# A fused linear-attention and feed-forward kernel: the first two chunks of a batch as one unit with two neighbouring tokens per partition

## The chip, the cores and the metric

The kernel runs on one core of one Trainium2 chip. The metric is the device time in microseconds of one execution. The core has TensorE (matmuls; in the profile PE, and PEld for its weight loads), VectorE (DVE), ScalarE (ACT), GpSimd (POOL) and SyncE (SP), which work side by side and wait for each other by semaphores, and 16 DMA engines that move data between device memory and the on-chip memory. Matmuls write to eight accumulator banks, from which VectorE or ScalarE copy.

## The reference

Two stages follow each other. The first is a recurrence over 768 tokens for 4 batches and 8 heads of 48 channels, all inputs fp32:

```
state = zeros((B, H, D, D))
for t in range(S):                       # S = 768, B = 4, H = 8, D = 48
    cur   = einsum('bhd,bhe->bhde', u * k[t], v[t])
    y[t]  = einsum('bhd,bhde->bhe', r[t], state + cur)
    state = w[t][:, :, :, None] * state + einsum('bhd,bhe->bhde', k[t], v[t])
```

The second takes y as 3072 tokens of 384 features and multiplies: `a = x @ w1`, `b = x @ w2`, `h = (a * b) @ w3`, `out = h @ w_out`, with a hidden width of 1024. The decay w lies between 0.8 and 0.95.

## The kernel before

The tokens of a batch are cut into six chunks of 128. Inside a chunk the recurrence is done as matmuls: with the running sum of log w over the chunk (`cs`, a matmul with a triangular matrix LT), k is scaled by exp(-sum) and r by exp(+sum), both are transposed so that channels lie on partitions, their product (`m`) is masked to earlier tokens (`msk`, or a copy and a select, `mcp` and `maff`), and multiplied with v (`yi`). The state that came into the chunk adds its part (`ys`), the token's own term is a row sum (`rk`, `ruk`, `dg`) times v (`dv`), added by VectorE (`yb`) or by a matmul with the identity (`yd`, for units in Y_PE). At the end of a chunk the state becomes (old state + k^T v) times the chunk's decay (`kv`, `T`, `S`, and a bf16 copy `Sb`).

A unit is one chunk of one or two batches, as listed in `UNITS` by chunk, first batch and number of batches; before there are thirteen, the first two of one batch. The tokens of the chunk lie on the 128 partitions, batches and heads side by side. `loads` (L337 to L354) brings r, k, v and w of a unit with four transfers; a row of one head and token is 48 fp32 values, 192 bytes. GpSimd's queue converts r, k and v to bf16 on the way; unit 0 comes unconverted over the queues of SP and ScalarE and is cast (`rc`, `kc`, `vc`, L349). In the units of the set RAW the sums are formed in transposed order by matmuls too (`csT`, L493) and r is transposed as it was loaded (`trw`, L505, then `KRw`, L510); in the others r is scaled first (`iw`, `rw`, `KRr`). Transposes are matmuls with the identity, or transfers on SP's queue where the unit stands in DMA_R, DMA_K or DMA_Y.

The feed-forward stage needs `w34 = w3 @ w_out`, built in eight pieces during the start (`wt`, `w3Te`, `wm`, `w34e`). Each unit's y, transposed as `xT`, is a block: `a` and `b` (L729) in four groups, ScalarE copies a (L734), VectorE multiplies (L739), and `o` (L745) gives 128 output rows, copied (L750) and stored by SP (L755).

The order of all work is written out by hand in `ORDER`, as names with an engine; each engine takes its own in that order and waits inside it. `BANKS` gives each product its accumulator bank. GpSimd's queue carries the loads after unit 0, the weights (w3 in quarters, w1 and w2 in halves, wo whole) and some computing, in the order of the list; a transfer of this queue waits for the landing of the one eight before it. `warmN@n` puts n/4 matmuls with zeros into TensorE's queue. Up to the first FFN product the order of transfers on GpSimd's queue is:

```
win_2 rin_1 kin_1 vin_1 win_3 kin_3 kin_2 rin_2 rin_3 w3_0 w3_1 wo win_4 vin_3 vin_2 w3_2 win_5 rin_4 w1_1
kin_4 rin_5 w2_1 kin_5 w1_0 win_6 w2_0 ...
```

Of the kernel before, what the change touches and what calls it, by code (L numbers as in the profile page):

```python
# [13 lines left out]
UNITS = [(0, 0, 1), (0, 1, 1), (0, 2, 2), (1, 0, 2), (1, 2, 2), (2, 0, 2), (2, 2, 2), (3, 0, 2), (3, 2, 2), (4, 0, 2),  # L14
    (4, 2, 2), (5, 0, 2), (5, 2, 2)]
# [13 lines left out]
RAW = {0, 1, 2, 3, 6}  # L29
N_PSUM = set()  # L30
DEPTH = {}
BLOCKS = [(0,), (1,), (2,), (3,), (4,), (5,), (6,), (7,), (8,), (9,), (10,), (11,), (12,)]
ROW_PC = {10}
DMA_R = {7, 8, 9, 10, 11, 12}
DMA_K = {8, 9, 10, 11, 12}
DMA_Y = {8, 9, 10, 11, 12}
PE_DIAG = set()
F32_IN = {0}
POOL_MASK = {(2, 0), (4, 1), (7, 1), (9, 1)}
Y_PE = {0, 1}  # L40
# [23 lines left out]
ORDER = """
zeros@DVE kin_0@ACT win_0@SP padlw@DVE ones@DVE win_1@ACT u@SP padpx@DVE I128@POOL padkr@DVE table@ACT rin_0@SP
padr@POOL vin_0@ACT win_2@POOL kc_0@DVE LT@POOL ln_0@ACT rin_1@POOL warm0@34 csT_0@PE cs_0@PE kin_1@POOL rc_0@DVE
ne_0@ACT vin_1@POOL ln_1@ACT KRk_0@DVE uc@DVE et_0@ACT warm2@13 trk_0@PE mask@DVE win_3@POOL cs_1@PE vc_0@ACT warm4@3
cc_1@PE csT_1@PE trw_0@PE cc_0@PE kin_3@POOL ln_2@ACT ne_1@ACT warm6@20 cs_2@PE kin_2@POOL et_1@ACT rk_1@DVE warm0@3
cc_2@PE pc_1@ACT ub@PE KRk_1@DVE trw_1@PE rk_0@DVE ue@ACT trk_1@PE rin_2@POOL pc_0@ACT ne_2@ACT ruk_0@DVE trke_0@DVE
padet@DVE KRw_1@DVE rin_3@POOL KRw_0@DVE ln_3@ACT warm0@29 m_0_0@PE w3_0@POOL kv_0@PE kv_1@PE msk_0_0@DVE trke_1@ACT  # L70
w3_1@POOL warm2@6 csT_2@PE S_0@DVE m_1_0@PE et_2@ACT dg_0@DVE wo@POOL dv_0@DVE pc_2@ACT win_4@POOL ruk_1@DVE warm0@12
csT_3@PE dg_1@DVE cs_3@PE KRk_2@DVE cc_3@PE vin_3@POOL msk_1_0@DVE pc_3@ACT trk_2@PE ne_3@ACT et_3@ACT vin_2@POOL
rk_2@DVE trw_3@PE dv_1@DVE yi_1_0@PE trw_2@PE trke_2@DVE w3_2@POOL yi_0_0@PE yd_1@PE KRk_3@DVE yd_0@PE ybc_1@ACT
win_5@POOL KRw_3@DVE ybc_0@ACT warm0@7 yt_1@PE trk_3@PE Sb_0@ACT KRw_2@DVE xT_1@ACT wt_1_0@PE rin_4@POOL trke_3@ACT
S_1@DVE wt_1_1@PE ruk_2@DVE m_2_0@PE m_2_1@PE Sb_1@ACT mcp_2_0@ACT wt_0_0@PE msk_2_1@DVE wt_0_1@PE w1_1@POOL m_3_1@PE
w3Te_0@ACT wt_2_0@PE msk_3_1@DVE yt_0@PE wt_2_1@PE xT_0@ACT m_3_0@PE w3Te_1@ACT maff_2_0@DVE warm2@1 ys_3@PE wt_3_0@PE
dg_2@DVE wt_3_1@PE rk_3@DVE ruk_3@DVE kin_4@POOL warm7@16 wm_1@PE msk_3_0@DVE wm_0@PE w3Te_3@DVE ln_4@ACT rin_5@POOL
dg_3@DVE w34e_1@ACT wm_3@PE iw_4@ACT w3Te_2@DVE w2_1@POOL w34e_0@DVE yi_3_0@PE dv_3@POOL w34e_3@ACT cs_4@PE yi_3_1@PE
e_4@ACT yi_2_0@PE wm_2@PE ne_4@ACT dv_2@POOL yb_3@DVE yi_2_1@PE w34e_2@DVE kv_3@PE kv_2@PE kin_5@POOL yb_2@DVE
wt_4_0@PE cc_4@PE wt_4_1@PE pc_4@ACT wt_5_0@PE w3Te_4@DVE yt_3@PE w1_0@POOL yt_2@PE xT_3@ACT S_2@DVE wt_5_1@PE wm_4@PE  # L80
win_6@POOL w3Te_5@DVE ln_5@ACT Sb_2@ACT cs_5@PE rw_4@DVE w2_0@POOL wm_5@PE e_5@ACT T_3@DVE KRr_4@DVE xT_2@ACT S_3@DVE
trr_4@PE iw_5@ACT w34e_4@DVE win_7@POOL cc_5@PE a_2_3@PE pc_5@ACT trre_4@ACT a_1_1@PE KRk_4@DVE vin_4@POOL a_2_2@PE
w34e_5@ACT a_3_3@PE asb_2_2@ACT rw_5@DVE kin_6@POOL trk_4@PE ne_5@ACT KRr_5@DVE a_0_1@PE trke_4@ACT rk_4@DVE a_3_2@PE
ruk_4@DVE asb_1_1@ACT w3_3@POOL trr_5@PE asb_0_1@ACT b_1_1@PE asb_2_3@ACT b_2_2@PE KRk_5@DVE win_8@POOL b_2_3@PE
rk_5@DVE abT_2_2@DVE b_0_1@PE abT_2_3@DVE asb_3_2@ACT trk_5@PE vin_5@POOL abT_0_1@DVE a_2_1@PE abT_1_1@DVE b_3_2@PE
asb_2_1@ACT trke_5@DVE m_4_0@PE ln_6@ACT win_9@POOL m_4_1@PE trre_5@DVE a_0_0@PE mcp_4_1@ACT msk_4_0@DVE a_1_0@PE
cs_6@PE rin_6@POOL abT_3_2@DVE asb_1_0@ACT b_0_0@PE asb_0_0@ACT ruk_5@DVE cc_6@PE ne_6@ACT a_3_1@PE dg_4@DVE b_1_0@PE
pc_6@ACT kin_7@POOL ln_7@ACT abT_0_0@DVE a_3_0@PE asb_3_1@ACT abT_1_0@DVE asb_3_3@ACT b_2_1@PE dv_4@POOL asb_3_0@ACT
cs_7@PE abT_2_1@DVE Sb_3@ACT m_5_0@PE ys_4@PE e_7@ACT maff_4_1@POOL msk_5_0@DVE kv_4@PE yi_4_0@PE a_2_0@PE rin_8@POOL
T_4@DVE cc_7@PE asb_2_0@ACT yi_4_1@PE csT_6@PE yb_4@DVE ne_7@ACT b_2_0@PE rin_7@POOL iw_7@ACT KRk_6@DVE wt_6_0@PE  # L90
yt_4@PE abT_2_0@DVE b_3_3@PE S_4@POOL pc_7@ACT xT_4@ACT dg_5@DVE wt_6_1@PE wt_7_0@PE win_11@POOL w3Te_6@ACT b_3_0@PE
abT_3_3@DVE a_4_1@PE abT_3_0@DVE ln_8@ACT kin_10@POOL wt_7_1@PE wm_6@PE et_6@ACT w3Te_7@DVE vin_7@POOL dv_5@DVE
asb_4_1@ACT cs_8@PE w34e_6@ACT vin_6@POOL ys_5@PE ln_9@ACT m_5_1@PE kv_5@PE msk_5_1@DVE yi_5_0@PE ne_8@ACT a_4_3@PE
win_10@POOL iw_8@ACT cc_8@PE rk_6@DVE yi_5_1@PE trw_6@PE asb_4_3@ACT KRk_7@DVE kin_8@POOL trk_6@PE pc_8@ACT yb_5@DVE
wm_7@PE trke_6@ACT KRw_6@DVE rin_11@POOL cs_9@PE rw_8@DVE w34e_7@ACT b_4_0@PE T_5@DVE e_8@ACT kin_9@POOL b_4_3@PE
ruk_6@DVE Sb_4@ACT rw_7@DVE b_3_1@PE KRr_7@DVE yt_5@PE rk_7@DVE o_0_0@PE win_12@POOL xT_5@ACT dg_6@DVE iw_9@ACT
ruk_7@DVE cc_9@PE a_4_0@PE ne_9@ACT KRr_8@DVE o_1_0@PE abT_4_3@DVE S_5@POOL asb_4_0@ACT dg_7@DVE ln_11@ACT rin_9@POOL
a_5_1@PE e_9@ACT abT_4_0@DVE trk_7@PE rin_10@POOL abT_3_1@DVE pc_9@ACT Sb_5@ACT o_2_0@PE asb_5_1@ACT trke_7@DVE
osb_1_0@ACT dv_7@POOL o_3_0@PE osb_2_0@DVE ln_10@ACT osb_0_0@ACT dv_6@ACT kv_6@PE m_6_0@PE T_6@DVE m_6_1@PE KRk_8@DVE
a_5_2@PE msk_6_1@DVE b_4_1@PE a_5_3@PE msk_6_0@DVE b_5_1@PE asb_5_2@ACT b_5_3@PE S_6@DVE osb_3_0@ACT abT_5_1@DVE  # L100
# [706 lines left out]
```

## Time and profile before

| | |
|---|---|
| three runs, us | 169.57, 169.60, 169.91 |
| median, us | 169.6 |
| the profiled execution's own time, us | 168.8 |
| its span, first to last instruction, us | 167.1 |
| TensorE busy | 156.5 us, 94% of the span |
| VectorE busy | 131.6 us, 79% |
| ScalarE busy | 94.9 us, 57% |
| GpSimd busy | 81.7 us, 49% |
| granted TensorE clock | 0.996 |
| DMA packets | 100791, of which 93057 under 512 bytes |

The profile is one execution. Times in it are microseconds from its first instruction. Rows of a timeline give start, duration, engine, source line and operation with its tiles, then a count of merged instructions, then in brackets the idle time of the engine before them and what ended it. Rows of a list by line give busy time, the mean in ns, and idle time with its causes. A busy TensorE is not TensorE at its peak: the matmul that ends a group counts with its latency.

### The profile page before, as it was taken

The page shows a single profiled execution, that of the slowest core. Times are in us where ns is not written, and L with a number is a line of the kernel's source. Part 1 is how long each engine was busy: PE and PEld are TensorE (multiplying, and loading weights), DVE is VectorE, ACT ScalarE, POOL GpSimd, SP SyncE. Part 2 cuts the span into 40 slices and gives each one's busy share as a digit, 9 for nine tenths or more (in the row PEclk, how much of TensorE's full clock was granted, in tenths as well). Part 3 has the DMA queues.
Part 4 walks back from the last instruction along what each step waited for, and adds up shares of the span by engine and source line. Part 5 has one row for each costly group of instructions (what it writes and reads, how often), then busy time and mean ns, then how long its engine had stood idle before and what let it go on. Part 6 is the DMA issues. An engine that isn't in the chain of part 4 may idle for free. (4 is left out here: it accounts for less than half of the span.)

```text
span 167.1 us, 4692 instructions
## 1 busy us (share of the span) xinstructions
PE 156.5 (94%) x1964; PEld 119.5 (72%) x1967; DVE 131.6 (79%) x212; ACT 94.9 (57%) x173; POOL 81.7 (49%) x82
## 2 busy tenths in 40 slices
PE   6699787999999999999999998999999999999991
PEld 2366664687998897876878785786688866678850
DVE  3448989679579898997899988799999989435730
ACT  3566494649948899879999565251721323025311
POOL 6999942798675999794001496909003110000000
PEclk9999999999999999999999999999999999999998
DMA  5999999999999999999989499993995540166014
GB/s 118 222 174 142 201 204 214 207 194 165 205 251 177 234 156 179 163 158 169 89 199 175 117 142 173 172 119 57 151 193 126 119 104 4 24 178 220 6 46 144
DMA packets 100791, 25.44 MB, mean 152 GB/s; under 512 B 93057, under 2 KB 98690, under 8 KB 100770
## 3 DMA queue, kind: packets, MB, share of 16 engines
q0 software_dynamic: 76192, 15.57, 105.3%
q1 hardware_dynamic: 21458, 8.99, 25.1%
q10 hardware_dynamic: 3120, 0.59, 1.9%
q8 instruction: 15, 0.25, 0.6%
q14 instruction: 6, 0.05, 0.1%
HBM read 27.79 MB, written 4.72 MB: 195 GB/s over the span
## 5 line engine op out<-in xcount | busy, mean ns | idle before, releaser
L729 PE MATMUL banks<-xT,w_bf 128*128 128x256 bf16 (+1 forms) x624 | 69.4, 264 | 0.6 <-DVE abT L739 0.4
L729 PEld LDWEIGHTS <-w_bf 128*128 128x128 bf16 x624 | 55.5, 98 | 8.2 <-issue 1.3
L734 ACT COPY a_sb<-banks 128x512 f32<-128x512 f32 x48 | 27.3, 594 | 24.5 <-PE banks L729 12.6
L739 DVE TENSOR_TENSOR abT<-a_sb,banks 128x512 bf16<-128x512 f32 x48 | 31.4, 679 | 4.5 <-ACT a_sb L734 2.3
L745 PE MATMUL banks<-w,abT 128*128 128x384 bf16 x192 | 33.8, 326 | 0.1
L610 DVE TENSOR_TENSOR Mbf<-banks,mask 128x1024 bf16<-128x1024 f32 x20 | 24.0, 1219 | 2.9 <-PE banks L591 2.3
L745 PEld LDWEIGHTS <-abT 128*128 128x128 bf16 x192 | 18.0, 97 | 11.2 <-issue 0.4
L579 POOL TENSOR_TENSOR dv<-vin,dg 128x768 bf16<-128x768 bf16 x8 | 11.9, 1498 | 15.0 <-DMA vin<-in_v_dram 9.7
L750 ACT COPY osb<-banks 128x384 f32<-128x384 f32 x14 | 6.8, 487 | 21.4 <-PE banks L745 13.1
L354 POOL DMA_DIRECT2D kin<-in_k_dram x12 | 13.7, 1144 | 4.4 <-DMA wo_bf<-in_moe_w_out_dram 3.3
L354 POOL DMA_DIRECT2D rin<-in_r_dram x12 | 13.8, 1156 | 3.1 <-DMA w_bf<-in_moe_w_dram 1.6
L655 DVE TENSOR_TENSOR yb<-banks,dv 128x768 bf16<-128x768 f32 x11 | 10.4, 955 | 6.2 <-PE banks L637 2.5
L354 POOL DMA_DIRECT2D win<-in_w_dram x11 | 13.2, 1200 | 3.1 <-ACT a_sb L734 1.5
L430 ACT ACTIVATE lw<-win 128x768 bf16<-128x768 f32 (+1 forms) x13 | 10.4, 800 | 6.7 <-DMA win<-in_w_dram 6.7
L354 POOL DMA_DIRECT2D vin<-in_v_dram x12 | 13.7, 1154 | 0.3 <-DMA w_bf<-in_moe_w_dram 0.2
L326 PE MATMUL banks<-zeros 128*128 128x512 bf16 (+3 forms) x37 | 11.2, 415 | 1.4 <-DVE zeros L257 1.3
L399 PE MATMUL banks<-wo_bf,w3T 128*128 128x384 bf16 x64 | 11.4, 326 | 0.8 <-DMA wo_bf<-in_moe_w_out_dram 0.8
L570 DVE TENSOR_REDUCE dg<-ruk 128x16 f32<-128x768 bf16 (+1 forms) x13 | 11.5, 883 | 0.1
L475 ACT ACTIVATE NEt<-banks 128x768 bf16<-128x768 f32 (+1 forms) x13 | 9.8, 757 | 0.9 <-PE banks L442 0.8
L560 DVE TENSOR_TENSOR rk<-rin,kin 128x768 bf16<-128x768 bf16 (+1 forms) x13 | 8.7, 667 | 2.0 <-DMA kin<-in_k_dram 2.0
L750 DVE COPY osb<-banks 128x384 f32<-128x384 f32 x10 | 5.5, 552 | 5.9 <-PE banks L745 3.0
L707 POOL TENSOR_TENSOR Sst<-Tst,pc 128x384 f32<-128x384 f32 x4 | 3.7, 933 | 11.8 <-DVE Tst L699 11.8
(89 smaller groups left out, 218.3 us busy)
## 6 DMA issues: line engine op xcount, KB each, us to landing
out_dram<-osb SPq DMA_DIRECT2D x24, 192.0 KB, 2.1
win<-in_w_dram POOLq DMA_DIRECT2D x11, 384.0 KB, 10.9
kin<-in_k_dram POOLq DMA_DIRECT2D x11, 192.0 KB, 9.9
rin<-in_r_dram POOLq DMA_DIRECT2D x11, 192.0 KB, 9.0
vin<-in_v_dram POOLq DMA_DIRECT2D x11, 192.0 KB, 9.9
w_bf<-in_moe_w_dram POOLq DMA_DIRECT2D x4, 512.0 KB, 11.7
w_bf<-in_moe_w_dram POOLq DMA_DIRECT2D x4, 384.0 KB, 11.8
wo_bf<-in_moe_w_out_dram POOLq DMA_DIRECT2D x1, 768.0 KB, 14.0
```

The costliest lines, as they stand in the source:

```text
L326: nc.tensor.matmul(banks[:, at, :k], lhsT=zeros[:, :C], rhs=zeros[:, :k], start=True, stop=True)
L354: QUEUE[eng].dma_start(dst, src)
L399: nc.tensor.matmul(one(f"wm{fi}")[:, :DM], lhsT=w3T[fi % 2][:, gi, :], rhs=wo_bf[:, gi, :], start=(gi == 0), stop=(gi == FI - 1))
L430: nc.scalar.activation(LW[:, :, :D], ww, Act.Ln)
L570: nc.vector.reduce_sum(dgs, ruks, axis=AX.X)
L579: e.tensor_mul(dvs, vv, dgs[:, :, None].to_broadcast([C, bh, D]))
L610: nc.vector.tensor_mul(Mbf[bank[f"M{t}_{b}"]], mview(), mask[:, None, None, :].to_broadcast([C, 2, HP, C]))
L729: nc.tensor.matmul(o[:, f, :], lhsT=wt[:, di, fi * P:(fi + 1) * P], rhs=x[:, di, :], start=(di == 0), stop=(di == DI - 1))
L734: copier(eng)(a_sb[bank[f"sa{ts[0]}_{g}"]], one(f"a{ts[0]}_{g}"))
L739: nc.vector.tensor_mul(ab[:, g * per:(g + 1) * per, :], sa.rearrange("p (f t) -> p f t", t=n), one(f"b{ts[0]}_{g}").rearrange("p (f t) -> ...
L745: nc.tensor.matmul(one(f"o{t}_{b}")[:, :DM], lhsT=ab[:, fi, k * C:(k + 1) * C], rhs=w34[:, fi, :], start=(fi == 0), stop=(fi == FI - 1))
L750: copier(eng)(osb[bank[f"so{t}_{b}"]], one(f"o{t}_{b}")[:, :DM])
```

## The change

The first two chunks of a batch become one unit of 256 tokens, four such units in all (set PAIR, units 0 to 3, one for each batch), in place of the five units of chunks 0 and 1. Partition p holds tokens 2p and 2p+1, so that partitions 0 to 63 are chunk 0 and 64 to 127 chunk 1, and a head's row of two tokens is 384 bytes. With that:

- The running sums take two matmuls for each parity of token (`cs`, with matrices BI and BS built by the step `pairs`), the transposed ones matmuls over half the partitions (`csT`, with Lx). The products `m` are formed in blocks of 64 by 64 (both chunks and both parities of the key), masked with Lx; `yi` works over 64 partitions.
- The state step from chunk 0 to chunk 1 is inside the unit: `kvz` and `Sz` make the state after chunk 0, `Sbz` writes it as a block-diagonal bf16 matrix Sbd, `ys` adds its part to chunk 1; then `kv`, `T`, `S` as before, for one batch at a time.
- The other units are renumbered (twelve in all, 4 to 11 for chunks 2 to 5), and ORDER, BANKS and the sets are written anew: units 5 to 11 use transfers for y's transposes (7 units, before 5), four units add their own term by matmul (before 2), the warm-up matmuls fall from 40 to 13 (`warm0@43`, then twice 4). The last output block is formed, copied and stored in two halves of 192 columns (HALVES).
- Unit 0 loads over SP and ScalarE as before, now two chunks of it, and so does win_1.

In the program TensorE has 2188 matmuls in place of 1967, and the shape of its tiles changes 72 times in place of 44. The order of transfers and computing on GpSimd's queue up to w2_0 is now:

```
kin_1 rin_1 win_2 w3_0 win_3 rin_2 vin_1 win_4 kin_3 kin_2 w3_1 dv_0 vin_2 wo rin_4 rin_3 win_5 kin_4 win_6 w3_2
dv_1 w1_1 w2_1 w1_0 rin_5 S_1 kin_5 vin_3 w2_0 ...
```

The core of the diff, with the line numbers left out:

```diff
-UNITS = [(0, 0, 1), (0, 1, 1), (0, 2, 2), (1, 0, 2), (1, 2, 2), (2, 0, 2), (2, 2, 2), ...
+UNITS = [(0, 0, 2), (0, 1, 2), (0, 2, 2), (0, 3, 2), (2, 0, 2), (2, 2, 2), ...
-RAW = {0, 1, 2, 3, 6}
+RAW = {0, 1, 2, 3}
+HALVES = {(11, 1)}
-DMA_R = {7, 8, 9, 10, 11, 12}
-DMA_K = {8, 9, 10, 11, 12}
-DMA_Y = {8, 9, 10, 11, 12}
+DMA_R = {5, 7, 9, 10, 11}
+DMA_K = {7, 8, 9, 10, 11}
+DMA_Y = {5, 6, 7, 8, 9, 10, 11}
-Y_PE = {0, 1}
+Y_PE = {0, 1, 2, 3}
+PAIR = {0, 1, 2, 3}
...
+        if t in PAIR:
+            for x in "wkrv":
...
+                src = ROW[x][b0, :, 0:2 * C, :].rearrange("h (p j) d -> p h (j d)", j=2)
...
+                for j in range(2):
+                    for z in range(2):
+                        nc.tensor.matmul(o[:, j, :], lhsT=BS if (j, z) == (0, 1) else BI,
+                                         rhs=LW[:, z * H:(z + 1) * H, :D], start=(z == 0), stop=(z == 1))
...
+                for q in range(HP if pair else 0):
+                    for e in range(2):
+                        for i in range(2):
+                            a = e * PAD
+                            nc.tensor.matmul(o[halves[i], e, q, :], lhsT=KRTs[a:a + PAD, 0, b * HP + q, halves[i]],
+                                             rhs=KRTs[a:a + PAD, 1, i * HP + q, :], start=True, stop=True)
...
+                for b, key in enumerate(("kvz", "kv")):
...
+                        for h in range(H):
+                            a = (h % 2) * PAD
+                            for z in range(2):
+                                nc.tensor.matmul(o[a:a + PAD, h // 2, :], lhsT=KRs[halves[b], 0, z * H + h, :],
+                                                 rhs=vv[halves[b], 2 * h + z, :], start=(z == 0), stop=(z == 1))
+                @op(f"Sz_{t}")
+                def _(eng):
+                    nc.vector.tensor_mul(Sp, kvv("kvz"), PCb[:, :HP])
...
+                @op(f"Sbz_{t}")
+                def _(eng):
+                    for e in range(2):
+                        w = halves[e]
+                        copier(eng)(Bd[w, :, e, :], Sp[w])
...
+                        nc.tensor.matmul(ypair()[:, 1, 2 * q:2 * q + 2, :], lhsT=KRTs[:, 1, HP + q, :], rhs=Bd[:, q],
+                                         start=False, stop=True, skip_group_check=True)
...
+                    dst = out[row:row + C, col]
+                    if t in PAIR:
+                        dst = dst.rearrange("(p j) o -> j p o", j=2)
+                    QUEUE[eng].dma_start(dst, osb[bank[f"so{z}{t}_{b}"]][:, :col.stop - col.start])
```

More of the change, by code (lines that the diff above doesn't have):

```diff
@@ L63 @@
+sa9_2=1 a11_1=3 b10_1=6 sa11_1=1 b10_2=5 sa10_3=2 b11_1=2 a11_2=1 a10_0=3 b11_2=4 sa10_0=3 o9_1=6 sa11_2=3 b10_3=3
+so9_1=1 b11_3=0 b11_0=1 a11_3=6 o10_1=5 so8_0=2 sa11_3=3 a11_0=3 o9_0=4 sa11_0=3 o10_0=7 so10_1=1 so9_0=2 o11_0=1
+so10_0=3 oh11_1=3 so11_0=0 o11_1=0 soh11_1=2 so11_1=1
 """
 ORDER = """
-zeros@DVE kin_0@ACT win_0@SP padlw@DVE ones@DVE win_1@ACT u@SP padpx@DVE I128@POOL padkr@DVE table@ACT rin_0@SP
-padr@POOL vin_0@ACT win_2@POOL kc_0@DVE LT@POOL ln_0@ACT rin_1@POOL warm0@34 csT_0@PE cs_0@PE kin_1@POOL rc_0@DVE
@@ L67 @@
[L67 to L81, printed above, removed]
@@ L97 @@
[L97 to L100, printed above, removed]
-cs_10@PE asb_5_3@ACT a_4_2@PE st_3_0@SP st_1_0@SP px_10@ACT abT_5_3@DVE dtr_7@SP ys_6@PE kv_7@PE abT_4_1@DVE yi_6_0@PE
@@ new lines @@
+table@ACT LT@POOL padr@POOL pairs@DVE kin_1@POOL rin_1@POOL ln_1@ACT ln_0@ACT win_2@POOL warm0@43 cs_1@PE rc_0@ACT
+w3_0@POOL kc_0@DVE cs_0@PE win_3@POOL ne_1@ACT csT_1@PE uc@DVE ne_0@ACT cc_0@PE rin_2@POOL csT_0@PE KRk_1@DVE et_1@ACT
+cc_1@PE KRk_0@DVE vin_1@POOL rk_1@DVE pc_1@ACT et_0@ACT trw_0@PE rk_0@DVE win_4@POOL trw_1@PE vc_0@ACT KRw_0@DVE
+trk_1@PE kin_3@POOL ub@PE pc_0@ACT trk_0@PE ln_2@ACT KRw_1@DVE kin_2@POOL trke_1@ACT trke_0@DVE warm7@4 csT_2@PE
+kvz_0@PE w3_1@POOL ue@ACT kv_0@PE Sz_0@DVE wt_1_0@PE et_2@ACT T_0@DVE m_0_0@PE ruk_0@DVE wt_1_1@PE Sbz_0@ACT
@@ new lines @@
+msk_0_0@DVE cs_2@PE w3Te_1@ACT m_0_1@PE S_0@DVE ln_3@ACT cc_2@PE msk_0_1@DVE yi_0_0@PE trw_2@PE ne_2@ACT kvz_1@PE
+dg_0@DVE pc_2@ACT yi_0_1@PE cs_3@PE ruk_1@DVE cc_3@PE dv_0@POOL ln_4@ACT ys_0@PE m_1_1@PE KRw_2@DVE ne_3@ACT Sz_1@DVE
+vin_2@POOL yd_0@PE pc_3@ACT Sbz_1@DVE m_1_0@PE ybc_0@ACT KRk_2@DVE wo@POOL msk_1_0@DVE warm7@4 trk_2@PE rin_4@POOL
+kv_1@PE trke_2@ACT wt_0_0@PE T_1@DVE cs_4@PE msk_1_1@DVE rin_3@POOL e_4@ACT m_2_0@PE cc_4@PE rk_2@DVE win_5@POOL
+wt_3_0@PE pc_4@ACT ne_4@ACT msk_2_0@DVE wt_3_1@PE wt_0_1@PE kvz_2@PE kin_4@POOL yt_0@PE Sz_2@DVE wt_2_0@PE padet@DVE
@@ new lines @@
+w3Te_0@DVE xT_0@ACT wt_2_1@PE win_6@POOL m_2_1@PE dg_1@DVE iw_4@ACT yi_1_0@PE Sbz_2@ACT mask@DVE yi_1_1@PE w3_2@POOL
+kv_2@PE ys_1@PE T_2@DVE dv_1@POOL wm_0@PE msk_2_1@DVE wm_1@PE ruk_2@DVE w1_1@POOL w34e_0@ACT w3Te_2@ACT dg_2@DVE
+w2_1@POOL yi_2_0@PE w34e_1@ACT rw_4@DVE w1_0@POOL yd_1@PE KRk_3@DVE yi_2_1@PE csT_3@PE rin_5@POOL dv_2@DVE wm_2@PE
+ln_5@ACT w3Te_3@DVE S_1@POOL ybc_1@ACT KRr_4@DVE kin_5@POOL ys_2@PE trk_3@PE w34e_2@ACT KRk_4@DVE cs_5@PE et_3@ACT
+trke_3@DVE yt_1@PE vin_3@POOL yd_2@PE xT_1@DVE e_5@ACT trw_3@PE w2_0@POOL ln_6@ACT cc_5@PE KRw_3@DVE wm_3@PE ybc_2@ACT
@@ L132 @@
+osb_11_1@ACT st_11_1@ACT
 """
@@ L289, in _ @@
             nc.vector.memset(x[:, :, :, D:], 0.0)
+        for x in Sbd:
+            nc.vector.memset(x, 0.0)
     if RAW:
```

357 lines of the change are left out of this document (234 added, 123 removed).

## The prediction

> **What bounds the kernel now.** I read the page first, then its busy tenths, then the stretches before, in and after the long row of FFN matmuls, then the chain of waits, then the timeline of the start.
>
> ```profile
> span 167.1 us, 4692 instructions
> PE 156.5 (94%) x1964; PEld 119.5 (72%) x1967; DVE 131.6 (79%) x212; ACT 94.9 (57%) x173; POOL 81.7 (49%) x82
> PE   6699787999999999999999998999999999999991
> PEclk9999999999999999999999999999999999999998
> DMA  5999999999999999999989499993995540166014
> ```
>
> TensorE is busy everywhere except in the first quarter and at the very end, the granted clock is full, and the DMA engines are full from the first slice on. The next view splits the span at the first FFN matmul (41.16 us) and at the end of the last one; its columns are time, then busy time of each engine, clock, DMA share.
>
> ```profile
> 0.00:41.16 41.16, 35.70 (x445) 23.71 (x449) 30.35 (x62) 24.51 (x43) 31.72 (x39) 1.00 1.68 184
> 41.16:163.54 122.38, 120.81 (x1525) 95.79 (x1521) 101.21 (x151) 69.95 (x130) 50.00 (x44) 1.00 1.24 143
> 163.54:167.10 3.56, 0.00 (x0) 0.00 (x0) 0.00 (x0) 0.48 (x1) 0.00 (x0) 0.83 0.31 110
> ```
>
> So the span is a start of 41.2, a stretch of 122.4 that TensorE fills, and a tail of 3.6 us. The chain of waits gives what a matmul costs when it follows others, and the tail:
>
> ```profile
> 140.31 0.33 PE banks L591 x8
> 140.64 0.42 PE banks L627 x32
> 141.06 0.31 PE banks L637 x8
> ...
> 142.67 0.20 PE banks L637 x8
> ...
> 147.83 10.49 PE banks L729 x96
> 158.32 5.21 PE banks L745 x32
> 163.54 0.02 issue
> 163.56 0.48 ACT osb L750
> ```
>
> L729 costs 10.49/96 = 0.109 us for 256 columns (so 0.055 for 128), L745 5.21/32 = 0.163 for 384, L637 0.20/8 = 0.025 for 48 columns; L627, in half-height tiles that overlap in pairs, 0.013. The same eight L637 take 0.31 after L627 and 0.20 among full-size matmuls: a change of tile shape costs about 0.1 us.
>
> Last, the timeline of the start. Each row is an instruction that waited for a transfer, so its time is a landing.
>
> ```profile
> 4.79 0.36 DVE L349 CAST kin<-abT 128x384 bf16<-128x384 f32 x1 [2.06 <-DMA abT<-in_k_dram]
> 7.45 0.51 ACT L349 CAST vin<-abT 128x384 bf16<-128x384 f32 x1 [0.24 <-DMA abT<-in_v_dram]
> 10.81 0.36 DVE L560 TENSOR_TENSOR rk<-rin,kin 128x384 bf16<-128x384 bf16 x1 [1.98 <-DMA kin<-in_k_dram]
> 13.36 0.84 ACT L430 ACTIVATE lw<-win 128x768 bf16<-128x768 f32 x1 [0.68 <-DMA win<-in_w_dram]
> 19.31 0.62 PE L505 MATMUL banks<-I,rin 128*128 128x128 bf16 x8 [0.72 <-DMA rin<-in_r_dram]
> 21.97 1.14 POOL L354 DMA_DIRECT2D rin<-in_r_dram  x1 [0.97 <-DMA w_bf<-in_moe_w_dram]
> 24.63 0.74 POOL L365 DMA_DIRECT2D w_bf<-in_moe_w_dram  x1 [1.52 <-DMA w_bf<-in_moe_w_dram]
> 28.43 4.06 PE L399 MATMUL banks<-wo_bf,w3T 128*128 128x384 bf16 x24 [0.81 <-DMA wo_bf<-in_moe_w_out_dram]
> 30.27 0.84 ACT L430 ACTIVATE lw<-win 128x768 bf16<-128x768 f32 x1 [3.50 <-DMA win<-in_w_dram]
> 41.19 0.98 PE L729 MATMUL banks<-xT,w_bf 128*128 128x256 bf16 x9
> ```
>
> With the order of issue in the code this is a price list of the one stream of transfers. Between win_3 (13.36) and rin_3 (19.31) lie kin_3, kin_2, rin_2, rin_3: 1.49 us each, for 2048 rows of 192 bytes. Quarters of w3 land at 21.97 and 24.63: 2.66. wo: 28.43 - 24.63 = 3.80. win_4, which keeps fp32: 1.84. Then come vin_3, vin_2, w3_2, win_5, rin_4 and w1_1 (three quarters of a w3 quarter's bytes: 2.0): 30.27 + 3 x 1.49 + 2.66 + 1.84 + 2.0 = 41.2, the very time of the first FFN matmul. So transfers set where the long stretch starts, and TensorE how long it lasts. TensorE's own work from the first L399 on says nearly the same: 28.43 + 12.3.
>
> **The change, part by part.** The sum is span = start of the FFN + stretch + tail.
>
> *Start: loads.* Units 0 to 3 now bring two chunks each, so unit 0 is five direct loads (with win_1) of 384 KB in place of 192. Two of today's have landed by 4.79, five by 7.45: 0.89 each, from a zero at 3.0. Twice the bytes in the same 1024 packets: between 0.89 (packets alone) and 1.78 (bytes alone); I take 1.15, near the low end because w3's quarter (1 MB in 2.66) would carry 384 KB in 1.00. They end at 3.0 + 5.75 = 8.8. A pair load on POOL's queue halves its packets (1024 of 384 bytes): between 1.00, w3's byte rate, and 1.49, no gain; a line through 192 bytes (0.73 ns a packet, all engines) and 4096 (10.4) gives 1.20 ns, so 1.23 us, a gain of 0.26. For win in pairs the same ratio: 1.5, between 1.0 and 1.84.
>
> Ahead of w1_1 POOL's order now has eight pair loads of r, k, v (all of units 1 to 3 but vin_3), win_2, win_3 in pairs, win_4, win_5, win_6 (5.52), rin_4, kin_4 (2.98), three quarters of w3 (7.98), wo (3.80), w1_1 (2.0). That is 8.8 + 9.84 + 3.0 + 22.28 = 43.9, against 41.2. The packets gained (10 x 0.3) don't pay for kin_4, win_6 and the second chunk of units 0 and 1, which moved ahead. Bounds: 39.7 with all low ends, 50 with all high ones.
>
> *Start: the other two bounds.* The same list puts wo at 31.4; from wm_0, the first product with it, to the first FFN matmul the program holds 11.2 to 12.2 us of TensorE work with its changes of shape: 42.6 to 43.6. For VectorE these groups of the list by line and shape, and one of ScalarE and one of POOL:
>
> ```profile
> L610 DVE TENSOR_TENSOR Mbf<-banks,mask 128x1024 bf16<-128x1024 f32 x20 | 24.0, 1219 | 2.9 <-PE banks L591 2.3 <-ACT KRT L556 0.4
> L570 DVE TENSOR_REDUCE dg<-ruk 128x16 f32<-128x768 bf16 x11 | 10.4, 944 | 0.0
> L480 DVE TENSOR_TENSOR KR<-kin,NEt 128x768 bf16<-128x768 bf16 x11 | 6.2, 563 | 1.6 <-ACT KRT L556 1.1 <-PE banks L691 0.4
> L564 DVE TENSOR_TENSOR ruk<-rk,u_bc 128x768 bf16<-128x768 bf16 x11 | 6.1, 553 | 0.1
> L556 DVE COPY KRT<-banks 128x1024 bf16<-128x1024 bf16 x3 | 2.0, 683 | 0.0
> L510 DVE TENSOR_TENSOR KRT<-banks,ETt 128x512 bf16<-128x512 bf16 x2 | 0.8, 421 | 0.1
> L704 DVE TENSOR_TENSOR Sst<-banks,pc 128x192 f32<-128x192 f32 x2 | 0.7, 348 | 0.0
> L712 ACT CAST Sbf<-Sst 128x192 bf16<-128x192 f32 x2 | 0.7, 360 | 0.0
> L579 POOL TENSOR_TENSOR dv<-vin,dg 128x768 bf16<-128x768 bf16 x8 | 11.9, 1498 | 15.0 <-DMA vin<-in_v_dram 9.7 <-issue 4.0 <-DVE dg L570 1.0
> ```
>
> From KRk_1 to w3Te_0, which wm_0 needs, VectorE's order has five masks (6.1), six KRw halves (2.5), seven small state steps (2.5), three each of KRk and rk (3.4), two ruk (1.1), one dg (0.9), two copies of 1024 columns (1.4): 18 us. KRk_1 waits for kin_1, about 11, so wm_0 is not before 29. All three bounds meet at 41 to 44; I keep 43.9.
>
> *Two POOL steps in the way.* dv_0 stands before vin_2 and wo, dv_1 before w1_1, w2_1 and w1_0; each is 1.5 us and waits for dg at the end of VectorE's chain. I cost them at nothing: issued loads are in flight for about ten microseconds, as the time from issue to landing shows; if that cover is gone they cost what dg is late.
>
> ```profile
> w_bf<-in_moe_w_dram POOLq DMA_DIRECT2D x4, 384.0 KB, 11.8
> ```
>
>
> *The stretch.* From the first FFN matmul on, the program holds 1518 matmuls before and 1486 after. FFN matmuls cost the same (94.1: 96 narrow L729 become 48 full ones, the last output is cut in two of 192 columns). Two w34 products and two transposes more are left (+3.1); work of the units falls by 1.3 to 2.7. Net +0.3 to +1.7: +1.0. Changes of tile shape go from 29 to 37: +0.8. VectorE's work is some 134 us by the prices of its list, of which about 36.5 stand ahead of the first FFN matmul, so 97 are left where 101.2 were; TensorE's waits there are 122.4 - 116.1 - 2.9 = 3.4, and I take 1.0 off. Stretch: 122.4 + 1.0 + 0.8 - 1.0 = 123.2.
>
> The Trainium skill, in TensorEngine Tiling (Array Packing), Key Properties, says that changing the tiling mode drains TensorE. The trace agrees, with 0.31 against 0.20 us for the same eight L637. By its table of Theoretical Speedup four 64x64 tiles would run at four times the rate of one, which no row here shows; by that the net work of the stretch would be its low end, +0.3 in place of +1.0.
>
> *At nothing.* Three more transposes on SP (21 to 24): their PE forms go, and SP has nothing else early. The warm-up matmuls (40 to 13) only fill waits. The masks Lx, Sbd's zeros and the wider casts lie before kin_1 lands. The eight small Sbz copies of state (0.36 each) on ScalarE and VectorE have TensorE's queue as cover; without it they add up to 3 us.
>
> *Tail.* The last copy and store move half the columns: 3.56 - 0.2 = 3.36 (0 to -0.5).
>
> Sum: 43.9 + 123.2 + 3.4 = 170.5 against 167.1, +3.4. The profiled run's own time is 168.8, the median 169.6; on the median that gives 173.0.
>
> **Rivals.**
> *A, faster: bytes alone count in the start.* If packets of 384 bytes run at w3's rate and unit 0's loads at 0.89, w1_1 lands at 39.7 and the span is 39.7 + 123.2 + 3.4 = 166.3: 168.7 on the median. It decides at an FFN start of 40.5. For it: the DMA row is full and most packets are small. Against it: 192 bytes already move at 264 GB/s against w3's 394, and the extra loads ahead of w1_1 remain.
> *B, much slower: TensorE's clock falls* where 27 fillers went.
>
> ```profile
> 1.26 3.81 PE L326 MATMUL banks<-zeros 128*128 128x512 bf16 x9 [1.26 <-DVE zeros L257]
> 11.95 1.73 PE L326 MATMUL banks<-zeros 128*128 128x512 bf16 x7
> ```
>
> The first nine cost 0.42 us each, later ones 0.25: TensorE begins at about half speed. Half speed for some 4 us of the start's work costs 4 us: 177. Against it: the program has 14 to 17 us of real work before wm_0 where it had 10. The Trainium skill, in TensorE: Matmul & The Clock Gate, part 1, says that an idle window of about 3.4 us halves the clock; the trace shows half speed only at the start.
> *C, slower still: POOL's queue.* If dg_0 and dg_1 come 3 us later than VectorE's chain allows, dv_0 and dv_1 hold wo and w1_1 back, the stream runs dry, and the FFN starts near 47: 176.
>
> **How the numbers follow.** Forecast 0.46 (170.5 to 175.5, by bounds of 41 to 46 on the FFN's start), A 0.27 (167 to 169.8), C 0.19, B 0.08. Runs spread over 0.2%, so about 0.3 us is no change: faster 0.24 and same 0.03 from A; the forecast's low edge gives 0.01 and 0.02; slower 0.70. The range runs from A's better half, 166.8, to 177.8, past B and C's centres, leaving about 0.1 at either end.
>
> **What would show it.** Right: the first L873 at 43 to 45, wo's first product near 31, about 123 us from there to the last L894, a tail of 3.3. Wrong: a first L873 before 40.5, pair loads landing 1.0 us apart, or much less than 3.4 us of waits in the stretch. A digit below 9 in PEclk after the first slices would be B; POOL idle before dv, waiting for dg, with a DMA row that thins near 25 or 35 us, C.

## The result, and the profile after

The changed kernel takes 194.7 us against 169.6: a ratio of 1.149, with a 95% interval of 1.138 to 1.159. I had forecast 173.0, and the top of my range was 177.8. It got slower, as I said, but by 25.1 us and not by 3.4. Two of its four runs, 197.1 and the profiled 198.75, were in a slower state of the chip, so the times here and in the experiments are medians of the others (here 193.8 and 195.7, with spans of 191.7 and 193.5), and some 3 to 5 us of the span below belong to that state.

From the page of the changed kernel: span, busy times, busy tenths of TensorE, granted clock, DMA.

```profile
span 196.7 us, 5176 instructions
PE 166.9 (85%) x2187; PEld 124.1 (63%) x2188; DVE 133.0 (68%) x229; ACT 102.4 (52%) x186; POOL 72.2 (37%) x77
PE   7579876999999996979969349942999998799993
PEclk9979999999999999999978966997599999999999
DMA  5999999999999999999989992949438263612124
```

The start looks as before, but for a clock of 7 tenths in its third slice. The hole is past the middle: digits of 3, 4, 4 and 2 for TensorE, and a clock of 5 to 7 in and behind them. In these four slices the DMA row reads 9, 9, 4 and 9, yet the page's row of GB/s has only 80, 100, 50 and 180 there, where the first nine slices have 138 to 266: much counts as under way, and little moves. The three stretches, split as before at the first and at the end of the last FFN matmul (time, busy time of PE, PEld, DVE, ACT, POOL, clock, DMA share, GB/s):

```profile
0.00:44.91 44.91, 37.08 (x702) 25.43 (x704) 33.56 (x74) 30.40 (x47) 30.21 (x41) 0.96 1.35 204
44.91:193.73 148.82, 129.86 (x1489) 98.62 (x1486) 99.44 (x156) 71.70 (x140) 41.97 (x36) 0.94 1.13 110
193.73:196.70 2.97, 0.01 (x1) 0.00 (x0) 0.00 (x0) 0.32 (x1) 0.00 (x0) 0.96 0.39 132
```

Start 44.9 (forecast 43.9), tail 3.0 (forecast 3.4), stretch 148.8 where I had 123.2. TensorE idles 19.0 us of it (before 1.6) and is busy 9 us longer for about the same work, at a clock of 0.94. The chain of waits names what the idle time waited for (start, length, what):

```profile
63.95 11.76 DMA KRT<-KR
...
95.03 5.50 DMA KRT<-KR
...
104.35 11.43 DMA xT<-yb
...
122.44 7.79 SPq L630
...
130.28 6.18 DMA xT<-yb
...
163.27 6.31 DMA out_dram<-osb
```

All of these are transfers that SP issues. The first two, at 63.95 and 95.03, begin before any store. The timeline of SP's queue shows what stands around them (L615 and L630 transpose r and k, L844 y; L908 is a store):

```profile
98.75 0.65 SPq L908 DMA_DIRECT2D out_dram<-osb  x1
99.50 4.24 SPq L844 DMA_TRANSPOSE xT<-yb  x3
103.79 0.51 SPq L908 DMA_DIRECT2D out_dram<-osb  x1
104.35 1.76 SPq L844 DMA_TRANSPOSE xT<-yb  x1
...
121.31 1.07 SPq L908 DMA_DIRECT2D out_dram<-osb  x2
122.44 7.79 SPq L630 DMA_TRANSPOSE KRT<-KR  x1
```

In the order of the code the stores at 98.75, 103.79 and 121.31 are st_2_0, st_2_1, st_3_0 and st_0_0: all of them stores of paired units. The transfer of 11.43 us stands right behind st_2_1; the transpose that kept SP for 7.79 us, where others take 1.2, right behind st_3_0 and st_0_0. The last of the chain, the ordinary store st_6_0 at 163.27, stands right behind st_3_1.

### The profile page after: what moved, and what is told of

Its sections match the earlier page's. It is cut to its first block, busy times and chain, and to the rows that moved or that the text cites. A ratio compares the mean times of both kernels' runs of the same rounds, so it can differ in the third digit from the quotient of the medians.

```text
span 196.7 us, 5176 instructions
## 1 busy us (share of the span) xinstructions
PE 166.9 (85%) x2187; PEld 124.1 (63%) x2188; DVE 133.0 (68%) x229; ACT 102.4 (52%) x186; POOL 72.2 (37%) x77
## 4 chain that ended last, share of the span: by engine, by line
PE 40%; DMA 30%; DVE 12%; SPq 7%; ACT 5%; issue 3%; POOL 2%; ACTq 0%; DVEq 0%; POOLq 0%
PE banks L873 21%; PE banks L894 11%; DMA xT<-yb 9%; DMA KRT<-KR 9%; DVE Mbf L706 5%; DMA win<-in_w_dram 5%; SPq L630 4%; DMA abT<-in_r_dram 4%; DMA out_dram<-osb 3%; SPq L844 2%; DVE abT L883 2%; DVE Tst L795 1%; PE banks L636 1%; SPq L908 1%; ACT NEt L537 1%
## 5 line engine op out<-in xcount | busy, mean ns | idle before, releaser
L873 PE MATMUL banks<-xT,w_bf 128*128 128x256 bf16 x576 | 75.4, 284 | 13.8 <-DMA xT<-yb 8.9
L873 PEld LDWEIGHTS <-w_bf 128*128 128x128 bf16 x576 | 56.6, 101 | 25.1 <-issue 13.9
L878 ACT COPY a_sb<-banks 128x512 f32<-128x512 f32 x48 | 27.4, 594 | 43.6 <-PE banks L873 31.4
L894 PE MATMUL banks<-w,abT 128*128 128x384 bf16 (+1 forms) x200 | 35.7, 329 | 0.0
L894 PEld LDWEIGHTS <-abT 128*128 128x128 bf16 x200 | 19.6, 100 | 12.6 <-issue 2.5
L706 DVE TENSOR_TENSOR Mbf<-banks,mask 128x1024 bf16<-128x1024 f32 x12 | 14.5, 1216 | 2.1 <-PE banks L685 2.1
L901 ACT COPY osb<-banks 128x384 f32<-128x384 f32 (+1 forms) x13 | 5.9, 470 | 19.1 <-DMA out_dram<-osb 11.6
L901 DVE COPY osb<-banks 128x384 f32<-128x384 f32 (+1 forms) x12 | 6.4, 537 | 12.0 <-PE banks L894 8.8
L658 DVE TENSOR_REDUCE dg<-ruk 128x16 f32<-128x768 bf16 x12 | 11.3, 945 | 0.1
L537 ACT ACTIVATE NEt<-banks 128x768 bf16<-128x768 f32 x12 | 9.7, 813 | 2.6 <-PE banks L498 2.6
L706 DVE TENSOR_TENSOR Mbf<-banks,Lx 128x1024 bf16<-128x1024 f32 x8 | 9.7, 1217 | 0.0
L436 PEld LDWEIGHTS <-w3T 128*128 128x128 bf16 x64 | 5.8, 97 | 5.5 <-DMA wo_bf<-in_moe_w_out_dram 1.6
L685 PE MATMUL banks<-KRT 64*128 64x128 bf16 x128 | 6.0, 221 | 3.5 <-DVE abT L883 1.6
```

The lines of the kernel that those rows point to most:

```text
L436: nc.tensor.matmul(one(f"wm{fi}")[:, :DM], lhsT=w3T[fi % 2][:, gi, :], rhs=wo_bf[:, gi, :], start=(gi == 0), stop=(gi == FI - 1))
L537: nc.scalar.activation(dst, cs_view(), Act.Exp, scale=-1.0)
L658: nc.vector.reduce_sum(dgs, ruks, axis=AX.X)
L706: nc.vector.tensor_mul(Mbf[bank[f"M{t}_{b}"]], mview(), m[:, None, None, :].to_broadcast([C, 2, HP, C]))
L873: nc.tensor.matmul(o[:, f, :], lhsT=wt[:, di, fi * P:(fi + 1) * P], rhs=x[:, di, :], start=(di == 0), stop=(di == DI - 1))
L878: copier(eng)(a_sb[bank[f"sa{ts[0]}_{g}"]], one(f"a{ts[0]}_{g}"))
```

## The experiments

Three theories. S: the store of a paired unit is carried by few DMA engines, because the change gave it an outermost dimension of two rows, and what needs these engines next waits. L: transposes by transfer that the change moved forward meet GpSimd's loads. K: TensorE's clock is a cause and not a consequence. Each experiment is compared with runs of the kernel before on the same chip (169.1 to 169.5 us).

**The store in halves.** Each pair store becomes two, one for each row of a pair, with 64 partitions outermost.

```diff
+                    src = osb[bank[f"so{z}{t}_{b}"]][:, :col.stop - col.start]
                     if t in PAIR:
                         dst = dst.rearrange("(p j) o -> j p o", j=2)
-                    QUEUE[eng].dma_start(dst, osb[bank[f"so{z}{t}_{b}"]][:, :col.stop - col.start])
+                        for j in range(2):
+                            QUEUE[eng].dma_start(dst[j], src[j * 64:j * 64 + 64])
+                        return
+                    QUEUE[eng].dma_start(dst, src)
```

> The changed kernel, with each of the eight stores of units 0 to 3 issued as two stores of 64 partitions each (even rows, then odd rows) in place of one whose outermost dimension is the two rows of a pair. The bytes and the packets are the same; SP has eight issues more. Theory S (a store that is cut in two by its outermost dimension is carried by two DMA engines, 64 packets of some 77 ns each, 5 us, and what stands behind it on SP's ring waits for those two engines): the waits of the chain behind the first store at 98.75 us (11.43 for xT, 7.79 of SP's queue for L630, 6.18 for xT, 6.31 for a store; 31.7 in all) go for the most part; 168 to 178 us. Theory L (the transposes by transfer lose against the loads that run at the same time, from 64 us on): the same time within 3 us, 193 to 199. Theory K (TensorE's granted clock is the cause, not the consequence): the same time too.

Measured: 182.9 us, ratio 1.078 (1.072 to 1.085). Nearly half of the loss, 11.8 of 25.1 us, is gone with nothing but the form of eight stores. That is less than S expected (168 to 178), and L and K expected none.

**Unit 5's r on TensorE, alone and with the halves.** `dtr_5@SP` goes; `trr_5@PE trre_5@ACT` come. In these two kernels the copy stands ahead of unit 3's last use of the same KRT buffer, so unit 3's ys uses the wrong r; the amount of work is the same.

```diff
-DMA_R = {5, 7, 9, 10, 11}
+DMA_R = {7, 9, 10, 11}
...
```

> The changed kernel, with unit 5's scaled r transposed on TensorE (eight transposes into a free bank and a copy on ScalarE) in place of SP's first transfer, at 63.95 us. Theory L (transposes beside GpSimd's loads): the wait of 11.76 us for KRT at 63.95 goes, 0.6 us of TensorE work comes; 183 to 190 us, and the loads behind it land sooner too. Theory S (stores on two engines): the first store is issued at 98.75, long after, so the gaps from 98 to 140 us stay; some of the wait of 11.76 was covered by other matmuls (TensorE was busy for 10.87 of the 11.0 us from 64 to 75), so no more than 3 us are gained: 192 to 197.

> Both edits together: stores in halves of 64 partitions, unit 5's r transposed on TensorE. Theory S: as with the stores alone, 168 to 178, and 1 to 3 us less than that. Theory L: as with unit 5's transpose alone, 183 to 190. If each of the two causes holds a share of its own, the two gains add up.

Measured: 197.4 us (1.158 to 1.170) alone and 185.4 us (1.084 to 1.099) with the halves. Taking the transfer at 64 us away gains nothing, although it led the chain for 11.76 us. The 185.4 lies in the range that L gave, but it is the halves that bring it there: they reach 182.9 without this edit. L's main instance falls; the clean form of this edit comes below.

**The form of the store alone, in the kernel before.** This is the test that has nothing else of the change in it.

```diff
-                QUEUE[eng].dma_start(out[row:row + C, :], osb[bank[f"so{t}_{b}"]])
+                dst = out[row:row + C, :]
+                if t < 5:
+                    dst = dst.rearrange("(p j) o -> j p o", j=2)
+                QUEUE[eng].dma_start(dst, osb[bank[f"so{t}_{b}"]])
```

> The kernel before, and nothing of the change but the form of the store: the eight stores of units 0 to 4 (the first two chunks of all batches) are written with the two rows of a pair as the outermost dimension, as the changed kernel does it, so their 128 rows land at exchanged places of their 128-row block of the output. Theory S: transposes and stores behind them on SP's ring wait some 5 us each time; 175 to 190 us. Theory L and theory K: as the kernel before, 169 to 171.

Measured: 199.1 us, ratio 1.177 (1.170 to 1.184): eight stores of the same bytes cost 29.7 us, more than S expected (175 to 190). The page of this kernel has the same hole, and its clock falls with it:

```profile
PE   7697989999999998995396045859999998699992
PEclk9999999999999999999669555767999999799999
```

With that K falls as the main cause: nothing was done to TensorE's work here, and its clock over the stretch went from 1.00 to 0.89. The waits of ScalarE for a free output buffer, first in the kernel before and then in this one (us in total, times, longest):

```profile
ACT osb L750 <- DMA out_dram<-osb: 8.3, 1, 8.3
```

```profile
ACT osb L750 <- DMA out_dram<-osb: 28.3, 5, 9.5
```

So the slow stores hold up two things: the transposes behind them, and the output buffers.

**Four rows, sixteen rows.** The same edit with j=4 and with j=16.

> The kernel before, with the same stores written with four rows as the outermost dimension. If that sets the number of engines: four engines, 32 packets of 77 ns each, 2.5 us a store in place of 4.9, so a loss of a third to a half of the 29.7 us that two rows cost, 176 to 185 us. If only the scatter or only the special case of two mattered: as with two rows, or as before.

> The kernel before, with the stores of units 0 to 4 written with sixteen rows as the outermost dimension (rows j, j+16, ... of a block of 128) in place of two: the same bytes, packets and issues, and the rows of a block again land at exchanged places. If the outermost dimension sets how many of the 16 DMA engines carry a store, all 16 do: as the kernel before, 169 to 171 us. If it is the scattered rows that cost: as with two rows, 195 to 201.

Measured: 183.1 us with four (1.075 to 1.084), 168.9 us with sixteen (0.995 to 1.001). The cost of the eight stores is 29.7, 13.6 and -0.6 us for an outermost dimension of 2, 4 and 16. The scatter of the rows is the same in all three; only the outermost number differs. The cost falls by about half from two to four, and is within the noise at sixteen. The median time from issue to landing of SP's transposes follows; in order the kernel before, and two, four and sixteen rows:

```profile
KRT<-KR SPq DMA_TRANSPOSE x11, 3.9
```

```profile
KRT<-KR SPq DMA_TRANSPOSE x11, 11.5
```

```profile
KRT<-KR SPq DMA_TRANSPOSE x11, 9.6
```

```profile
KRT<-KR SPq DMA_TRANSPOSE x11, 4.3
```

In the changed kernel the same row reads

```profile
KRT<-KR SPq DMA_TRANSPOSE x10, 13.8
```

The trace does not name the engine of a packet, but it settles how many work at once. The first two of these stores follow each other in all four kernels. Their 256 packets of 1536 bytes took 1.25 us in the kernel before, then 9.40, 5.13 and 1.74 us with two, four and sixteen rows; the durations of the packets add up to 14.3, 2.1, 4.0 and 13.3 times these spans, so that many were in flight at a time. The packets of SP's queue on the four pages, in the same order, say it once more:

```profile
q1 hardware_dynamic: 21458, 8.99, 25.1%
```

```profile
q1 hardware_dynamic: 21346, 8.99, 26.9%
```

```profile
q1 hardware_dynamic: 21362, 8.99, 27.8%
```

```profile
q1 hardware_dynamic: 21458, 8.99, 26.1%
```

There are 112 and 96 fewer with two and four rows, 14 and 12 for each of the eight stores, all of them packets of 4 bytes, as if each engine that carries a store adds one: 2, 4 and 16 engines. The changed kernel shows the same, with 1.8 to 2.1 packets in flight during its pair stores and 4.1 to 5.8 us for one that runs alone, where an ordinary store takes 0.5 to 0.7; two in a row took 8.4 and 10.3 us, still with 2.0 in flight, as if both went to the same two engines. The Trainium skill has the rule, in DMA: Bandwidth & Descriptors, section Why a DMA increments its semaphore by 16 and not by 1: a transfer is spread over the largest number of engines up to 16 that divides the slowest dimension of both sides. The runs agree with it, at 29.7, 13.6 and -0.6 us and at 2.1, 4.0 and 13.3 packets in flight.

**Another ring.** The eight pair stores in their old form, issued by ScalarE (`st_0_0@ACT` and so on).

> The changed kernel, with its eight pair stores in their form of two outermost rows, but issued by ScalarE on a ring of its own. Theory S in the narrow sense (what waits is what stands behind the store on the same ring): nearly all is gained that the stores in halves gave, 180 to 186 us. Theory S in the wide sense (the two engines are taken, whatever the ring): the transposes still need these two engines, and share them with the store; a part is gained, 186 to 194. Theories L and K: 194 to 199.

Measured: 195.1 us (1.143 to 1.162): no gain at all, less than even the wide form of S expected. By itself this would fit L or K; the kernel before with pair stores speaks against both. The chain of waits of this kernel has the same pieces:

```profile
92.74 7.46 DMA KRT<-KR
...
103.57 8.10 DMA out_dram<-osb
...
120.55 10.40 DMA xT<-yb
```

So it isn't the place in SP's ring that counts. What the two rings share, engines and output buffers, is still taken; which of the two costs more, this run doesn't tell.

**The natural order, made elsewhere.** The copy that fills xT puts the tokens back in order, and the pair store becomes one block of 128 rows.

```diff
+                if pair:
+                    copier(eng)(x[:, :, :nb * C].rearrange("p d n -> p (d n)").rearrange("p (a t j) -> p a j t", t=64, j=2),
+                                ytv().rearrange("p d n -> p (d n)").rearrange("p (a j t) -> p a j t", j=2, t=64))
+                    return
...
-                    if t in PAIR:
-                        dst = dst.rearrange("(p j) o -> j p o", j=2)
```

> The changed kernel, with the tokens of units 0 to 3 put back into their natural order by the copy that fills xT (it writes with a stride of two columns), so each of their stores is one block of 128 rows, one issue on SP, as all other stores. Theory S (stores whose outermost dimension is two rows are carried by two engines and hold up SP's ring): at least what the stores in halves gave (182.9 us), and a little more, since SP saves eight issues of 0.58 us that stood ahead of transposes between 96 and 121 us: 177 to 182. If the strided copy is dear (five copies of 0.55 to 0.8 us, doubled), up to 3 us of that is lost. Theory L (transposes beside loads) and theory K (clock): nothing beyond the stores in halves, 182 to 184.

> The kernel with the order restored in xT, and unit 5's r transposed on TensorE, now behind unit 3's last use of the same buffer. If SP's transfer at 64 us beside GpSimd's loads still costs something of its own, 1 to 4 us less than without this edit; if it is covered by other matmuls, the same or up to 1 us more, for 0.6 us of TensorE work and one copy of ScalarE's.

Measured: 179.3 us (1.047 to 1.063), and with unit 5's r on TensorE 179.0 (1.052 to 1.060): 15.7 of the 25.1 us are back, and the transfer at 64 us is hidden. Against the halves the natural order saves another 3.6 us; eight issues on SP of about 0.58 us are 4.6. The stretches of the kernel with both edits, and its row for KRT:

```profile
0.00:44.67 44.67, 35.96 (x701) 24.23 (x703) 32.88 (x74) 30.46 (x47) 30.30 (x41) 1.00 1.36 207
44.67:173.90 129.23, 124.38 (x1498) 97.24 (x1494) 100.31 (x156) 72.13 (x141) 41.69 (x36) 0.99 1.10 124
```

```profile
KRT<-KR SPq DMA_TRANSPOSE x9, 3.6
```

Its stretch is 19.6 us shorter than that of the changed kernel's profile: 14.1 of idle time and 5.5 of TensorE's busy time, with a clock of 0.99 in place of 0.94. It is still 6.9 us longer than before the change (4.85 us of idle time against 1.57, and 3.6 us more busy time), the start 3.5 us. All that follows starts from this kernel and looks for these 10 us.

**y of units 5 and 6, then r of unit 7, on TensorE.** `DMA_Y` loses 5 and 6; then `DMA_R` loses 7 as well.

> The kernel with the natural order in xT and unit 5's r on TensorE (179.1 us), and y of units 5 and 6 transposed on TensorE again (12 transposes and two copies on ScalarE) in place of four transfers on SP, which has 19 transposes then, where the kernel before has 21. If the transposes that the change moved to SP cost the rest of the stretch: 3 to 5 us less, 174 to 176. If they are hidden: 1 us more, for TensorE's 1.0 us.

> The kernel with natural order in xT, unit 5's r and the y of units 5 and 6 on TensorE (178.4 us), with unit 7's r on TensorE as well: SP then has 18 transposes, three fewer than the kernel before, and its first transfer since the start is unit 7's k. If SP's first transposes beside the last loads cost the remaining waits (5.5 us of chain at 92.7 us in the kernel with the natural order): 174 to 177 us. If TensorE's waits there only move elsewhere: 178 to 180.

Measured: 178.2 us (1.041 to 1.057) and 179.5 us (1.057 to 1.065). With 18 transposes on SP, three fewer than the kernel before has, nothing is gained. L falls for the rest too.

**wo, then vin_2 and wo, ahead of dv_0 on GpSimd's queue.** In the changed kernel GpSimd waited for dg_0, and wo was late:

```profile
22.01 1.65 POOL L667 TENSOR_TENSOR dv<-vin,dg 128x768 bf16<-128x768 bf16 x1 [7.29 <-DVE dg L658]
...
24.54 0.88 POOL L410 DMA_DIRECT2D wo_bf<-in_moe_w_out_dram  x1
```

```profile
33.10 2.77 PE L436 MATMUL banks<-wo_bf,w3T 128*128 128x384 bf16 x16 [1.48 <-DMA wo_bf<-in_moe_w_out_dram]
```

> The kernel with the natural order in xT and unit 5's r on TensorE (179.1 us), and wo's load issued ahead of dv_0 on GpSimd, at about 14.5 us in place of 23. If GpSimd's wait for dg_0 (6.0 us, in the timeline) holds back wo and with it the first product of w34 at 32.3 us and the FFN's start at 44.7: wo lands some 4 us sooner, the FFN starts 1 to 3 us sooner, 176 to 178.5 us. If TensorE's other work or the later loads set the start anyway, the same within 0.7 us.

> The kernel with the natural order in xT and unit 5's r on TensorE (179.1 us), with both vin_2 and wo issued ahead of dv_0, in the 6 us in which GpSimd waits for dg_0. If that wait leaves the stream of transfers dry: wo lands by 29, vin_2 is no longer late, the FFN starts at 41 to 43.5 in place of 44.7; 175.5 to 178 us. If the stream stays full and only the order in it changes: the FFN starts at 44.5 to 46.5 and the time is 178.5 to 181.

Measured: 180.7 us (1.059 to 1.073), which neither side expected, and 180.0 us (1.057 to 1.072). With wo alone in front, vin_2 becomes late; with both in front, the first product of w34 waits for no transfer and still starts at 32.6:

```profile
31.30 0.43 PE L762 MATMUL banks<-vin,KR 64*64 64x48 bf16 x16 [2.52 <-DMA vin<-in_v_dram]
```

```profile
32.63 2.76 PE L436 MATMUL banks<-wo_bf,w3T 128*128 128x384 bf16 x16
```

With both in front the FFN starts at 44.15 in place of 44.67. That is less than the start varies by itself: the kernel with 18 transposes on SP has the same program up to there as the one of 44.67, and starts its FFN at 46.08, since its clock fell under the first products of w34 (11 of them took 3.64 us in place of 1.96). GpSimd's wait is real, and no gain from taking loads out from behind it is shown.

**Fillers.** Warm-up matmuls (fillers) are added in the waits of the kernel with the natural order and unit 5's r on TensorE (`warm6@28 cc_0@PE` and four like it), and taken from the kernel before. By the counts of TensorE's instructions it is 17 more and 31 fewer, not the 18 and 28 of the expectations.

> The kernel with the natural order in xT and unit 5's r on TensorE (179.1 us), with 18 warm-up matmuls more, put where TensorE waits: before cc_0, trw_2, kvz_1 and wm_0 in the start, and before unit 7's product with its transposed k. Theory K for the rest (TensorE's clock, granted at 0.96 to 0.99 over whole runs where the kernel before has 1.00, is lost behind waits that no filler covers): the mean clock rises to 1.00 and the time falls by 1.5 to 4 us, to 175 to 177.5. If the fall of the clock is only a trace of the waits: the same, 178 to 181.

> The kernel before, without its warm-up matmuls but the first nine (34 quarters), so 28 fillers fewer; nothing else is changed. Rival B of the prediction (the clock falls where the fillers went): the granted clock of the start falls below 1.0 and the time rises by 1.5 to 4 us, 171 to 173.5. If the real work of the start keeps the clock: 169 to 170.

Measured: 180.7 us (1.061 to 1.076) and 171.2 us (1.007 to 1.015). The clock row with the added fillers is full, the time is not shorter:

```profile
PEclk9999999999999999999999999999999999999999
```

So K falls for the rest as well. The kernel before without its fillers is 1.9 us slower, in the range given to rival B. Its page shows a clock of 1.00, but in its trace the clock is on record from 20.4 us on only, and until then its matmuls are slow: eight L493 take 1.03 us where they took 0.61. So the fillers did keep the clock up there. The FFN still starts at 41.05, and the two microseconds are idle time in the stretch (3.55 against 1.57, with 120.8 us of work in both); why they arise there stays open. With the clock full, the FFN matmuls of the stretch take about what they took before; first the kernel before, then the one with added fillers, in the list of groups by line:

```profile
L729 PE MATMUL banks<-xT,w_bf 128*128 128x256 bf16 (+1 forms) x624 | 69.4, 264 | 0.6 <-DVE abT L739 0.4
L399 PE MATMUL banks<-wo_bf,w3T 128*128 128x384 bf16 x16 | 2.9, 326 | 0.0
```

```profile
L877 PE MATMUL banks<-xT,w_bf 128*128 128x256 bf16 x576 | 70.1, 273 | 4.5 <-DMA xT<-yb 4.5
L436 PE MATMUL banks<-wo_bf,w3T 128*128 128x384 bf16 x32 | 5.9, 326 | 0.3 <-DVE Mbf L706 0.3
```

w34's products in the stretch are 3.0 us more, and the units' own work is about 1 us less. What is left beside the work is idle time: 6.9 us of this stretch, 3.9 to 8.8 in the other kernels with mended stores, whichever wait is taken away; it only moves. None of these kernels beats the kernel before.

## Why the prediction was wrong

*The step that failed* is the paragraph "At nothing". It counted SP's transposes, 21 to 24, and cleared them with "SP has nothing else early". It priced no store at all, although the diff rewrites the store of units 0 to 3 with `"(p j) o -> j p o"`. These eight stores have the same bytes, the same 1536-byte rows and the same count of issues, so I passed over them; they cost 29.7 us in the kernel before and 15.7 in the changed one, because an outermost dimension of two lets two packets run at a time. The transposes themselves were in fact free once the stores were mended: three edits that took them off SP one after the other moved the time by -0.3, -0.8 and +1.3 us, where the runs of one such kernel lie up to 2.6 us apart.

*Start, 43.9.* Measured 44.9, and 44.2 to 46.9 in the later kernels that use the right r. I had wo at 31.4 and the first product with it not before 29 by VectorE's chain: it came at 33.1, after a wait of 1.48 us for wo. From there to the FFN it took 11.8 us, inside the 11.2 to 12.2 that I had counted. That other bounds lie close by was right: with wo out of the way the product still came at 32.6.

*Stretch, 123.2.* Without the pair stores it is 127 to 132. The sum had +1.0 of work and +0.8 for changes of tile shape. The kernel with wo in front ran its stretch at a full clock:

```profile
46.88:174.24 127.36, 123.15 (x1497) 96.15 (x1494) 100.49 (x156) 72.08 (x141) 39.54 (x34) 1.00 1.05 122
```

TensorE is busy 123.15 us against 120.8 before; 0.6 of that are the eight transposes of unit 5's r that the experiment added, so the change's own part is about +1.7, where I had +1.8. How much of it is tile shape no run took apart, and so none shows the fourfold rate of 64x64 tiles, which is an estimate from the Trainium skill's table in TensorEngine Tiling (Array Packing), Theoretical Speedup (twice the rate for each of the two small dimensions). The other term, VectorE's relief of -1.0, had the wrong sign. I took it off waits of 3.4 us, where the view I showed has TensorE idle for only 1.57. VectorE has 99.4 us of work in the stretch where I had 97 (101.2 before), and TensorE's idle time grew by 2.3 us or more in every kernel with mended stores, in most of them waiting above all for transposes by transfer.

*Tail, 3.36.* Measured 2.97: right in direction, 0.4 us better.

*Rivals.* A needed an FFN start before 40.5; none of the changed kernels came before 44.1, so bytes alone don't set the start. B: the clock fell in the start too (7 tenths in the third slice, 0.96 over the start), and that can cost: the FFN starts at 44.2 to 45.0 in the three kernels with a full clock there, at 44.2 to 46.9 in the others; the changed kernel's 44.9 holds little of it. In the stretch it fell to 0.94, as the consequence of idle time, and with a full clock the time stayed. C: GpSimd did wait 7.3 us for dg_0, and the loads moved ahead of that wait gained nothing of the time. The kernels with the natural order, 178.2 to 180.7 us, lie just above my range. In the best understood of them, at 179.0, 3.5 of the 10 us over the kernel before are the start, 2.4 TensorE's work with the eight added transposes, about 1.2 its clock of 0.99, 3.3 idle time in the stretch, and the tail gives 0.6 back. Why the waits there only move stays open.

## What to carry to other kernels

When a diff changes only the shape of a transfer, price it as a new transfer: same bytes and same packet size say nothing if the outermost dimension shrinks. Here 2 and 4 were slow, and 16, 64 and 128 were not. Put the partitions outermost, and where data must change places, do it in a copy that is made anyway. When a whole chain waits on a queue, look at what stands just ahead of the late transfer, since here the row that waited was not the row that cost.

## What the runs showed of the hardware that I had not expected

- Eight stores of 192 KB cost 29.7, 13.6 and -0.6 us with an outermost dimension of 2, 4 and 16. The first two of them together took 9.40, 5.13 and 1.74 us, with 2.1, 4.0 and 13.3 packets in flight.
- Moving them to ScalarE's ring gained nothing (195.1 against 194.7 us).
- A slow transfer on SP holds up SP itself: a transpose that takes 1.2 us to issue took 7.79 behind two pair stores.
- TensorE's clock falls behind gaps that another unit makes, so a slow store also costs TensorE speed: the granted clock went from 1.00 to 0.89 over the stretch, and longer busy time is 11 of the 32 us by which the stretch grew in the kernel before with pair stores (131.8 us busy against 120.8, idle 23.0 against 1.6).
- Copies with a stride of two columns cost little: 1.02 us each for the four copies of xT, where the changed kernel without the stride took 0.55 (VectorE) and 0.80 (ScalarE).
- A clock of 1.00 on the page need not hold for the first microseconds: the kernel before without its fillers reads 1.00, and its matmuls took up to 1.7 times as long until 20 us.
